# mLSTM attention, router, MoE and MLP in one kernel: the outputs, gates, rows and states of an attention unit taken up one unit later, its turn two units later, and the router's tables built ahead of all units

## The chip, the cores and the metric

The kernel runs on one core of a Trainium2 chip. The metric is the device time of one execution in microseconds (us), as the median of several runs; lower is better. Engines are named as in the profile: PE multiplies matrices (PEld is its weight load, which overlaps), DVE is the vector engine, ACT the scalar engine, POOL the general engine, SP issues most of the loads.

## The reference

Three stages stand one behind the other. The first is a recurrent attention over 4 batches, 8 heads, 768 steps and head size 40, the second a mixture of 8 experts with a capacity, the third a two-layer network.

```python
for t in range(S):                                   # attention
    m_new = np.maximum(f_gate[:, :, t] + m, i_gate[:, :, t])
    f_stab = np.exp(f_gate[:, :, t] + m - m_new); i_stab = np.exp(i_gate[:, :, t] - m_new)
    C = f_stab * C + i_stab * einsum('bhd,bhe->bhde', vt, kt)
    n = f_stab * n + i_stab * kt
    denom = np.maximum(np.abs(einsum('bhd,bhd->bh', n, qt)), 1.0)
    y[:, :, t] = sigmoid(o_gate[:, :, t]) * einsum('bhde,bhe->bhd', C, qt) / denom
logits = x @ w_gate                                  # x: 3072 tokens x 320
# tokens go to experts in the order of falling logits, 384 to an expert
out[mask] = np.maximum(x[mask] @ w1[e], 0.0) @ w2[e]
h = x @ w_in                                         # 320 -> 2048
return np.where(h > 0, h, np.exp(np.minimum(h, 0)) - 1) @ w_out
```

(Broadcast indices are left out.)

## The kernel before

The attention works chunk by chunk: 12 chunks of 64 steps, and for each chunk two pairs of batches, which makes 24 units, `u` = 0 to 23. A unit holds 64 steps of two batches (the two halves of the 128 partitions) and all 8 heads. `Attention.run` (from L455) is one Python loop over the units, and since the schedule is manual each engine executes its instructions in the order in which this loop issues them. That order is the subject of the change.

In one turn of the loop, in order:

- PE: `values(u)` (L368, 32 small matmuls of P and the values into the PSUM tile pO), interleaved with `scores(u+2)` (L283, into pS); then `recall(u)` (L382, the state times the queries, added onto the same pO), interleaved with `state(u)` (L394, new state increments into pC); then `turn(u-1)`: three 128x128 transposes of the output rows x of the unit before into pX (L438), which ACT copies to xT (L440).
- For the next unit: `scan` (DVE, W, L309), `factors` (POOL, vp and qt, L316 and L319), `opens` (ACT, sg is the sigmoid of the output gate, L354), `weigh` (DVE, P is pS times W, L359).
- `gates(u)`: DVE forms 1/max(|n·q|, 1) from the last column of pO (rd, L414, L416, L418), POOL multiplies sg by it (L420). Then `fade(u+1)` on POOL (kt, L328, and the faded state, L330), `decay(u+2)` on PE (pF and pD, L291; ACT copies pD to db, L302).
- `logits(u-1)`: PE multiplies xT by the router's gate weights (L448, six passes), ACT copies 8 columns into L (L449). `add_state(u)`: DVE adds pC to the state C (L405).
- `rows_out(u)`: DVE forms x = pO · sg (L427), ACT pads it (L429) and issues two DMAs of the rows to the DRAM buffer xd (L432, queued on ACT).

Between these stand *fills*: `fl(i)` issues a number of conversion pieces of the later network's weights `w_in` (list FP, from unit 4 on) and of steps of the router's early work (list EP). A piece of `w_in` is loaded by SP into cx; ACT takes an absolute value (cg, L868), DVE does three bit operations on it (cF, L873, L877, L880, the last one with cg as input), then ACT and POOL (L926, L928) or ACT and DVE (wis, L932 to L938) split it into two parts. The router's early work (`Router.early`, DVE, L608 to L628) takes the logits of six units' rows at a time for a first digit of the threshold search; `Router.tables` makes constant tables with iotas on POOL (L517 to L543) and shifts on DVE (from L547).

PSUM holds eight tiles here: pO and pS have two buffers each, pF, pD, pC and pX one each. A matmul that writes a buffer waits until the reader of what stood in it is done.

After the last unit come `turn(23)`, `logits(23)` and the last early work; then the router's search over all 3072 tokens, a chain of DVE and PE steps that needs all of L, and with its first indices the gather of rows from xd. The rest of the span, from about 200 us on, is the experts and the network, ordered by a planner; the change doesn't touch that.

Of the kernel before, what the change touches and what calls it, by code (L numbers as in the profile page):

```python
# [8 lines left out]
F32 = mybir.dt.float32  # L9
# [8 lines left out]
NS, NU = 12, 24  # L18
# [16 lines left out]
class Plan:  # L35
# [3 lines left out]
    def __init__(self):  # L39
        self.n = 0  # L40
        self.todo = []
        self.reset()
# [39 lines left out]
    def next(self):  # L82
        self.due(min(self.todo)[0])
# [30 lines left out]
class Attention:  # L114
# [3 lines left out]

    def __init__(self, nc, tc, consts, qk, vk, ig, fg, wg, xd, L, ident):
        self.nc, self.tc, self.qk, self.vk, self.xd, self.L, self.ident = nc, tc, qk, vk, xd, L, ident  # L120
# [50 lines left out]
        for x in self.CS[0] + self.CS[1]:  # L171
            G.memset(x[:, :, 41:], 0.0)
        self.dp = one.tile([96, S], BF, name="dp")
        self.isT = one.tile([128, NS, 16], F32, name="isT")
# [177 lines left out]
    def opens(self, u):  # L352
        sg = self.st["sg", u] = self.two.tile([128, 8, 40], F32, name="sg")
        self.nc.scalar.activation(sg, self.by_token(u, 2), AF.Sigmoid)  # L354
# [79 lines left out]
    def turn(self, u):  # L434
        x = self.st.pop(("x", u))
        p = self.st["T", u] = self.psum("pX", 1).rearrange("p h t -> p (h t)")
        for k in range(3):
            self.nc.tensor.transpose(p[:, k * 128:k * 128 + 128], x[:, k * 128:k * 128 + 128], self.ident)  # L438
        xT = self.st["xT", u] = self.two.tile([128, 3, 128], F32, name="xT")
        self.nc.scalar.activation(xT.rearrange("p k t -> p (k t)"), p[:, :384], AF.Copy)  # L440

    def logits(self, u):

        l = self.st.pop(("T", u))[:, 384:392]
        x = self.st.pop(("xT", u))
        for k in range(3):
            z = 128 if k < 2 else 64
            self.nc.tensor.matmul(l, x[:z, k], self.wg[:z, k], start=k == 0, stop=k == 2)  # L448
        self.nc.scalar.activation(self.L[:, :, u % 4 * 6 + u // 4], l, AF.Copy)  # L449
# [6 lines left out]
    def run(self, hook, fill):  # L456
        later = self.later()
        for u in range(NU):
            v, w = u + 1, u + 2
            fl = lambda i: ([fill() for _ in range(FP[i])] if u > FU else []) + [self.step() for _ in range(EP[i])]  # L460
            if u % 2 == 0 and u // 2 + 2 < NS:
                self.load_qk(u // 2 + 2)
                self.load_vk(u // 2 + 2)
            self.both(self.values(u), self.scores(w))
            self.both(self.recall(u), self.state(u))
            if u > 0:
                self.turn(u - 1)
            if v < NU:
                self.scan(v)
                self.factors(v)  # L470
                self.opens(v)
                self.weigh(v)
            fl(0)
            if u < 3:
                next(later, None)
            self.gates(u, fl)
            if v < NU:
                self.fade(v)
            fl(2)
            if w < NU:  # L480
                self.decay(w)
            if u > 0:
                self.logits(u - 1)
            self.add_state(u)
            fl(3)
            if u == NU - 1:
                while self.extra:
                    self.step()
            self.rows_out(u)
            fl(4)  # L490
            if u == 0:
                self.turn_gi(2, NS)
                self.keep_gi(2, NS)
            hook(u)
        self.turn(u)
        self.logits(u)
        hook(NU)
        self.es.close()


class Router:
# [9 lines left out]
    def tables(self):  # L511
# [33 lines left out]
        self.thr0 = stage.tile([128, 128], I32, name="thr0", bufs=1)  # L545
        m = stage.tile([128, 128], I32, name="tblt", bufs=1)
        V.tensor_scalar(jt, jt, 25, None, op0=ALU.logical_shift_left)  # L547
        yield
# [854 lines left out]
def kernel(ctx, tc, qk, vk, ig, fg, wg, w1a, w1b, w2a, win, wout, out):  # L1403
# [13 lines left out]
    sp = stage.enter_context(tc.tile_pool(name="cv", bufs=2))  # L1417
    at = Attention(nc, tc, consts, qk, vk, ig, fg, wg, xd, L, ident)

# [5 lines left out]
    def hook(u):  # L1425
        if u == FU:
            fill()
            fill()
        if u == 2:
            rt.__init__(nc, tc, consts, wk, L, sp, plan)  # L1430
            at.extra.append(rt.tables())
            at.step()
        if 4 <= u < 23 and u % 4 == 0:
            at.extra.append(rt.early(u // 4 - 1))
        if u == 22:
            at.extra.append(rt.early(5, 0, 2))
        if u == 23:
            at.extra.append(rt.early(5, 2, 3))
        if u == 24:
            while at.extra:  # L1440
                at.step()
            rt.dg = rt.digits(0)
            for _ in rt.early(5, 3, 4, rt.dg):
                pass
# [18 lines left out]
def _layout(i):  # L1463
# [21 lines left out]
    wg = i["moe_w_gate"][:, ::-1]  # L1485
    d["wg"] = np.concatenate([wg, np.zeros((64, 8), wg.dtype)]).reshape(3, 128, 8).transpose(1, 0, 2)
    d["w1a"] = i["moe_w1"][:, :256].reshape(2048, 1024)
# [22 lines left out]
```

## Time and profile before

| What | Value |
|---|---|
| median of 3 runs | 817.9 us (817.57 to 819.57) |
| the profiled execution's own time | 817.59 us |
| its span, first to last instruction | 815.8 us |
| mean granted TensorE clock | 0.925 of full |
| busy, share of the span: PE, DVE, ACT, POOL | 89%, 72%, 43%, 38% |
| attention's units by the first `values` matmul (L368) | 12.67 us (unit 0) to 157.09 us (unit 23) |

The busy shares are a mean over stages with different limits: PE's 89% comes from the long part behind 200 us. In the 24 units that the change reorders the shares are others and differ among themselves, so the rows further down are taken stage by stage. A stretch named by two units runs from the first `values` matmul of the one to that of the other. Where a row names "issue" as what was waited for, the profile shows nothing else that the engine waited for.

### The profile page before, as it was taken

Reading aid. Unit: us, or ns where it says so; the run is one execution under the profiler, and the core shown is the slowest. Engines: PE = TensorE matmul, PEld = TensorE weight load, DVE = VectorE, ACT = ScalarE, POOL = GpSimd, SP = SyncE. Lnnn points to the kernel's source line nnn. Section 1 sums busy time; section 2 is a strip of 40 time slices with the busy share of each in tenths; the row PEclk is TensorE's granted clock in tenths of the full one; section 3 lists DMA queues with packets and bytes.
Section 4 is the critical chain, followed back from the end, with each engine's and each line's share of the span. In section 5 each row is a group of like instructions: output and inputs, shape, how many; then the busy total and the mean of one; then the engine's idle time right before and its main releaser. Section 6 shows DMA issues by size and latency. Waiting matters only on the chain.

```text
span 815.8 us, 18330 instructions
## 1 busy us (share of the span) xinstructions
PE 729.8 (89%) x7355; PEld 681.9 (84%) x7355; DVE 586.1 (72%) x1616; ACT 348.5 (43%) x743; POOL 309.2 (38%) x358
## 2 busy tenths in 40 slices
PE   7788788836899799799999999999999999999995
PEld 5678678725788789789989988898999999999995
DVE  8697878777979976987897679867733942862542
ACT  5343334324356533543553255325533633742431
POOL 3687887626425631633134125213410601201001
PEclk8678787856999999999999999999999999999998
DMA  8766855135114202112123103200500410100000
GB/s 343 253 216 209 278 186 187 43 107 199 54 30 139 83 27 78 51 44 100 32 65 93 40 0 106 67 27 0 172 12 13 138 35 25 65 1 26 1 1 25
DMA packets 20757, 72.79 MB, mean 89 GB/s; under 512 B 3200, under 2 KB 7296, under 8 KB 19264
## 3 DMA queue, kind: packets, MB, share of 16 engines
q1 hardware_dynamic: 8336, 35.08, 12.6%
q0 software_dynamic: 8448, 31.73, 11.8%
q10 hardware_dynamic: 3888, 4.82, 2.1%
q8 instruction: 58, 0.95, 0.5%
q14 instruction: 27, 0.22, 0.1%
HBM read 62.96 MB, written 8.65 MB: 88 GB/s over the span
## 4 chain that ended last, share of the span: by engine, by line
PE 58%; DVE 21%; issue 8%; ACT 4%; DMA 4%; POOL 2%; ACTq 1%; SPq 0%; POOLq 0%; DVEq 0%
PE ph L1096 24%; PE acc L1234 5%; PE acc L1238 4%; PE acc L1235 4%; PE acc L1203 3%; PE acc L1205 3%; PE acc L1204 3%; DVE e L1149 2%; DMA xd<-x 2%; PE pr L727 2%; DVE ge L713 1%; DVE gl L980 1%; PE acc L1190 1%; PE pX L448 1%; DMA vk<-in_vk_dram 1%
## 5 line engine op out<-in xcount | busy, mean ns | idle before, releaser
L1234 PE MATMUL acc<-woh,gh 128*128 128x320 f32 x384 | 122.7, 320 | 0.0
L1238 PE MATMUL acc<-woh,gl 128*128 128x320 f32 x384 | 119.7, 312 | 0.0
L1235 PE MATMUL acc<-wol,gh 128*128 128x320 f32 x384 | 119.0, 310 | 0.0
L1149 DVE SCALAR_TENSOR_TENSOR e<-e,ph 128x384 f32<-128x384 f32 x128 | 69.9, 549 | 61.8 <-ACT e L1146 61.4
L1145 ACT ACTIVATE e<-ph 128x384 f32<-128x384 f32 x128 | 62.7, 489 | 116.3 <-PE ph L1096 112.0
L980 POOL TENSOR_TENSOR gl<-e,gh 128x384 fp32r<-128x384 f32 x33 | 34.8, 1057 | 164.3 <-DVE gh L974 132.3
L1096 PE MATMUL ph<-yh,wih 128*128 128x384 f32 x256 | 89.7, 351 | 0.4
L1096 PE MATMUL ph<-yh,wil 128*128 128x384 f32 x256 | 86.2, 337 | 0.0
L1113 ACT ACTIVATE gh<-ph 128x384 fp32r<-128x384 f32 x64 | 31.3, 491 | 121.9 <-PE ph L1096 120.7
L1244 POOL DMA_INDIRECT out_dram<-ot,idx x24 | 24.0, 1001 | 141.3 <-ACT ot L972 138.1
L1120 DVE SCALAR_TENSOR_TENSOR gl<-ph,gh 128x384 fp32r<-128x384 f32 x64 | 35.4, 556 | 56.8 <-ACT gh L1113 56.4
L1238 PEld LDWEIGHTS acc<-woh,gl 128*128 128x128 f32 x384 | 72.5, 189 | 0.6
L1234 PEld LDWEIGHTS acc<-woh,gh 128*128 128x128 f32 x384 | 72.8, 190 | 0.2
L1235 PEld LDWEIGHTS acc<-wol,gh 128*128 128x128 f32 x384 | 72.7, 189 | 0.0
L1146 ACT ACTIVATE e<-e 128x384 f32<-128x384 f32 x128 | 67.3, 526 | 4.0
L1096 PE MATMUL ph<-yl,wih 128*128 128x384 f32 x256 | 66.5, 341 | 0.0
L980 DVE TENSOR_TENSOR gl<-e,gh 128x384 fp32r<-128x384 f32 x95 | 57.3, 607 | 1.9
L1096 PEld LDWEIGHTS ph<-yh,wih 128*128 128x128 f32 x256 | 48.4, 189 | 4.5 <-ACT yh L1208 4.4
L1096 PEld LDWEIGHTS ph<-yh,wil 128*128 128x128 f32 x256 | 48.3, 189 | 0.0
L1096 PEld LDWEIGHTS ph<-yl,wih 128*128 128x128 f32 x256 | 46.4, 189 | 0.0
L1096 PE MATMUL ph<-xh,w1h 128*128 128x384 f32 x128 | 45.0, 352 | 0.2
L1203 PE MATMUL acc<-gh,w 128*128 128x384 f32 x128 | 44.6, 349 | 0.0
(269 smaller groups left out, 2023.5 us busy)
## 6 DMA issues: line engine op xcount, KB each, us to landing
vk<-in_vk_dram SPq DMA_DIRECT2D x12, 968.0 KB, 8.7
qk<-in_qk_dram SPq DMA_DIRECT2D x11, 1024.0 KB, 8.0
wx<-in_wout_dram SPq DMA_DIRECT2D x16, 320.0 KB, 2.8
xd<-x ACTq DMA_DIRECT2D x48, 96.0 KB, 3.7
cx<-in_win_dram SPq DMA_DIRECT2D x8, 512.0 KB, 4.4
qk<-in_qk_dram SPq DMA_DIRECT2D x2, 512.0 KB, 5.9
cx<-in_win_dram SPq DMA_DIRECT2D x4, 256.0 KB, 4.2
xg<-xd,idx POOLq DMA_INDIRECT x24, 3.3
```

Source lines behind the costliest of these rows:

```text
L980: (self.nc.vector if e == "d" else self.nc.gpsimd).tensor_tensor(out, x, y, op=ALU.subtract)
L1096: PE.matmul(p, w, x, start=k == 0, stop=k == 7)
L1113: nc.scalar.activation(h, p, AF.Relu)
L1120: nc.vector.scalar_tensor_tensor(l, p, 0.0, h, op0=ALU.max, op1=ALU.subtract)
L1145: nc.scalar.activation(e, p, AF.Relu, scale=-1.0)
L1146: nc.scalar.activation(e, e, AF.Exp, scale=-1.0)
L1149: nc.vector.scalar_tensor_tensor(e, e, -1.0, p, op0=ALU.add, op1=ALU.max)
L1203: PE.matmul(p, w[:, c], h, start=f == 0, stop=False)
L1204: PE.matmul(p, w[:, cl], h, start=False, stop=False)
L1234: PE.matmul(p, h[:, c], self.woh[:, f], start=f == 0, stop=False)
L1235: PE.matmul(p, h[:, c], self.wol[:, f], start=False, stop=False)
L1238: PE.matmul(p, l[:, c], self.woh[:, f], start=False, stop=f == 15)
```

## The change

In the turn of the loop for unit u, `add_state`, `gates` and `rows_out` are now those of unit u-1, `turn` and `logits` those of unit u-2; `add_state(u-1)` is the first thing in the turn. `values`, `recall`, `state`, `scan`, `factors`, `opens`, `weigh`, `fade` and `decay` stay. What is left over follows the loop: gates and rows of unit 23, then turn and logits of 22 and 23, the last one in a buffer of pS. sg gets a third buffer. The third transpose reads columns 192 to 319 of x rather than the padded columns 256 to 383, and the gate weights' rows are laid out to match. The iotas on POOL are issued while the attention is set up, before unit 0, and no longer in unit 2; each part of the router's early work starts one unit later.

```diff
@@ Attention.__init__
+        next(tables)
@@ opens
-        sg = ... self.two.tile([128, 8, 40], F32, name="sg")
+        sg = ... self.two.tile([128, 8, 40], F32, name="sg", bufs=3)
@@ turn
-        p = ... self.psum("pX", 1)
+        p = ... self.psum(*(("pX", 1) if u < NU - 1 else ("pS", 2)))
         for k in range(3):
-            transpose(p[:, k * 128:k * 128 + 128], x[:, k * 128:k * 128 + 128], self.ident)
+            c = min(k * 128, 192)
+            transpose(p[:, k * 128:k * 128 + 128], x[:, c:c + 128], self.ident)
@@ logits
-            z = 128 if k < 2 else 64
-            matmul(l, x[:z, k], self.wg[:z, k], start=k == 0, stop=k == 2)
+            z = 0 if k < 2 else 64
+            matmul(l, x[z:, k], self.wg[z:, k], start=k == 0, stop=k == 2)
@@ run
         for u in range(NU):
+            if u > 0:
+                self.add_state(u - 1)
...
             self.both(self.recall(u), self.state(u))
-            if u > 0:
-                self.turn(u - 1)
+            if u > 1:
+                self.turn(u - 2)
...
-            self.gates(u, fl)
+            if u > 0:
+                self.gates(u - 1, fl)
...
-            if u > 0:
-                self.logits(u - 1)
-            self.add_state(u)
-            fl(3)
-            if u == NU - 1:
-                while self.extra:
-                    self.step()
-            self.rows_out(u)
+            if u > 1:
+                self.logits(u - 2)
+            fl(3)
+            if u > 0:
+                self.rows_out(u - 1)
...
-        self.turn(u)
-        self.logits(u)
-        hook(NU)
+        self.gates(u, lambda i: self.step())
+        while self.extra:
+            self.step()
+        self.rows_out(u)
+        for k in (u - 1, u):
+            self.turn(k)
+            self.logits(k)
+            hook(k + 2)
@@ hook
-        if 4 <= u < 23 and u % 4 == 0:
+        if 5 <= u < 23 and u % 4 == 1:
             at.extra.append(rt.early(u // 4 - 1))
-        if u == 22:
+        if u == 23:
             at.extra.append(rt.early(5, 0, 2))
...
```

The order of the instructions at two places shows what that does. In its rows a tile's name carries a number that tells one buffer's use from the next, and the end names the engines or queues whose semaphores an instruction waits for.

The first place is DVE in unit 7. Before, pO_1163 is the output tile of unit 7 itself and x_1281 its rows:

```order
L309 SCALAR_TENSOR_TENSOR W_1235<-pF_1128,id8_135 128x512 [waits PE_49]
L359 TENSOR_TENSOR P_1242<-pS_1037,W_1235 128x512 [waits DVE_49]
L873 TENSOR_SCALAR cF_982<-cx_980 128x512 [waits DMAHW0_49]
L414 TENSOR_SCALAR rd_1246<-pO_1163 128x8 [waits PE_49]
L877 SCALAR_TENSOR_TENSOR cF_982<-cx_980,cF_982 128x512 [waits DVE_49]
L416 TENSOR_TENSOR rd_1246<-rd_1246,pO_1163 128x8 [waits DVE_49]
L418 RECIPROCAL rd_1246<-rd_1246 128x8 [waits DVE_49]
L405 TENSOR_TENSOR C11_143<-C11_143,pC_153 128x8x41 [waits PE_49,Pool_49]
L880 SCALAR_TENSOR_TENSOR cF_982<-cg_981,cF_982 128x512 [waits Activation_49]
L427 TENSOR_TENSOR x_1281<-pO_1163,sg_1113 128x320 [waits DMAHW3_49,DMAHW1_49,Pool_49]
```

After, pO_1006 is the output tile of unit 6, and x_1260 that unit's rows (its line numbers are 1 higher here, 8 higher in the conversions):

```order
L406 TENSOR_TENSOR C01_140<-C01_140,pC_184 128x8x41 [waits PE_49]
L310 SCALAR_TENSOR_TENSOR W_1214<-pF_1105,id8_135 128x512 [waits PE_49]
L360 TENSOR_TENSOR P_1221<-pS_1007,W_1214 128x512 [waits DVE_49]
L881 TENSOR_SCALAR cF_962<-cx_960 128x512 [waits DMAHW6_49]
L415 TENSOR_SCALAR rd_1225<-pO_1006 128x8
L885 SCALAR_TENSOR_TENSOR cF_962<-cx_960,cF_962 128x512 [waits DVE_49]
L636 TENSOR_TENSOR A_1093<-w8_163,a8_1092 128x32
L417 TENSOR_TENSOR rd_1225<-rd_1225,pO_1006 128x8 [waits DVE_49]
L419 RECIPROCAL rd_1225<-rd_1225 128x8 [waits DVE_49]
L888 SCALAR_TENSOR_TENSOR cF_962<-cg_961,cF_962 128x512 [waits Activation_49]
L428 TENSOR_TENSOR x_1260<-pO_1006,sg_953 128x320 [waits DMAHW7_49,DMAHW1_49,Pool_49]
```

The state's addition moved to the head, and rd no longer waits for PE. The reader that frees unit 6's output tile, x_1260, now stands at the end of unit 7 behind the conversion that waits for ACT; the tile that takes the same buffer is that of unit 8, whose `values` are PE's next instructions.

The second place is ACT at the end of the attention. Before, from the logits copy of unit 21 to that of unit 23:

```order
L449 ACTIVATE L_70<-pX_3101 128x8 [waits PE_49]
L429 ACTIVATE x_3126<-x_3126 128x64 [waits DMAHW7_49,DMAHW6_49,DVE_49]
L432 DMA xd_71<-x_3126 64x384 [waits Activation_49]
L432 DMA xd_71<-x_3126 64x384
L440 ACTIVATE xT_3168<-pX_3164 128x384 [waits PE_49]
L449 ACTIVATE L_70<-pX_3164 128x8 [waits PE_49]
L429 ACTIVATE x_3186<-x_3186 128x64 [waits DMAHW1_49,DMAHW0_49,DVE_49]
L432 DMA xd_71<-x_3186 64x384 [waits Activation_49]
L432 DMA xd_71<-x_3186 64x384
L440 ACTIVATE xT_3195<-pX_3191 128x384 [waits PE_49]
L449 ACTIVATE L_70<-pX_3191 128x8 [waits PE_49]
```

After, from the turned rows of unit 21 to the logits copy of unit 23:

```order
L442 ACTIVATE xT_3147<-pX_3143 128x384 [waits PE_49]
L451 ACTIVATE L_70<-pX_3143 128x8 [waits PE_49]
L430 ACTIVATE x_3159<-x_3159 128x64 [waits DMAHW7_49,DMAHW6_49,DVE_49]
L433 DMA xd_71<-x_3159 64x384 [waits Activation_49]
L433 DMA xd_71<-x_3159 64x384
L430 ACTIVATE x_3176<-x_3176 128x64 [waits DMAHW1_49,DMAHW0_49,DVE_49]
L433 DMA xd_71<-x_3176 64x384 [waits Activation_49]
L433 DMA xd_71<-x_3176 64x384
L442 ACTIVATE xT_3185<-pX_3181 128x384 [waits PE_49]
L451 ACTIVATE L_70<-pX_3181 128x8 [waits PE_49]
L442 ACTIVATE xT_3201<-pS_3197 128x384 [waits PE_49]
L451 ACTIVATE L_70<-pS_3197 128x8 [waits PE_49]
```

Behind PE's last `recall` there were two copies to xT and two to L, those of units 22 and 23; now there are three of each, and the pads and DMAs of units 22 and 23 stand ahead of the last two pairs.

## Rows read from the trace of the kernel before

**Rows 1.** The first line of the page.

```profile
span 815.8 us, 18330 instructions
```

**Rows 2.** Busy time of the engines in five stretches: units 0 to 3 and the first third of the next, then to unit 14, to unit 19, to unit 21, and the end of the attention. Columns: the window's start and end, its length, busy us of PE, PEld, DVE, ACT and POOL (with instructions), PE's granted clock, the DMA engines' share, GB/s.

```profile
12.67:46.67 34.00, 27.25 (x745) 25.50 (x742) 25.14 (x54) 15.33 (x35) 20.34 (x39) 0.72 0.71 255
46.67:117.76 71.09, 58.42 (x1685) 53.96 (x1684) 59.96 (x116) 27.12 (x71) 59.55 (x62) 0.76 0.71 234
117.76:143.46 25.70, 20.84 (x614) 18.99 (x613) 21.52 (x44) 10.82 (x27) 19.39 (x21) 0.80 0.58 198
143.46:157.09 13.63, 11.48 (x381) 10.48 (x380) 12.28 (x29) 5.43 (x16) 11.85 (x14) 1.00 0.20 48
157.09:167.00 9.91, 8.13 (x100) 7.04 (x100) 3.60 (x17) 1.96 (x7) 1.33 (x2) 0.55 0.18 42
```

**Rows 3.** What PE waited for from 42.67 us to 157.09 us (the start of unit 4 to that of unit 23): waiting line, releaser, us in total, times, longest us.

```profile
PE pC L394 <- POOL kt L328: 5.2, 6, 1.7
PE pO L382 <- issue: 4.8, 3, 2.4
PE pX L448 <- ACT xT L440: 2.1, 4, 1.0
PE pC L394 <- issue: 1.8, 2, 1.2
PE pD L291 <- issue: 1.7, 2, 1.0
PE pF L291 <- DVE W L309: 1.0, 2, 0.6
```

**Rows 4.** The same for DVE, in the same stretch.

```profile
DVE rd L414 <- PE pO L382: 6.5, 4, 3.5
DVE x L427 <- POOL sg L420: 3.8, 7, 0.7
...
```

**Rows 5.** The timeline of PE, ACT and DVE at the end of unit 7: start, length, engine, instruction, and in brackets the engine's idle time before it and its releaser.

```profile
65.89 0.55 PE L438 MATMUL pX<-ident,x 128*128 128x128 f32 x3
67.02 0.93 PE L448 MATMUL pX<-wg,xT 128*128 128x8 f32 x6
67.88 0.27 PE L368 MATMUL pO<-vp,P 64*64 64x64 f32 x2
...
66.48 0.49 ACT L440 ACTIVATE xT<-pX 128x384 f32<-128x384 f32 x1 [4.47 <-PE pX L438]
66.86 0.46 ACT L354 ACTIVATE sg<-vk 128x320 f32<-128x320 f32 x1
67.22 0.66 ACT L868 ACTIVATE cg<-cx 128x512 f32<-128x512 f32 x1
...
67.92 1.27 DVE L880 SCALAR_TENSOR_TENSOR cF<-cg,cF 128x512 int32<-128x512 int32 x1 [0.47 <-ACT cg L868]
69.11 0.48 DVE L427 TENSOR_TENSOR x<-pO,sg 128x320 f32<-128x320 f32 x1
```

**Rows 6.** The same at the end of unit 13.

```profile
105.57 0.66 ACT L868 ACTIVATE cg<-cx 128x512 f32<-128x512 f32 x1
...
106.26 1.01 DVE L880 SCALAR_TENSOR_TENSOR cF<-cg,cF 128x512 int32<-128x512 int32 x1 [0.58 <-ACT cg L868]
...
106.91 0.37 PE L368 MATMUL pO<-vp,P 64*64 64x64 f32 x2
```

**Rows 7.** The same at the end of unit 19.

```profile
142.92 0.63 ACT L934 ACTIVATE wis<-cF 64x512 fp32r<-64x512 f32 x1
...
143.96 1.01 DVE L938 TENSOR_TENSOR wis<-cF,wis 64x512 fp32r<-64x512 f32 x1
...
143.46 0.27 PE L368 MATMUL pO<-vp,P 64*64 64x64 f32 x2
```

**Rows 8.** The end of the attention. First five pieces of the chain that ended last, in order of time (start, length, what); then from the timeline, in its form, two instructions of DVE and the two DMAs on ACT's queue.

```profile
160.00 0.84 PE pX L438 x3
160.87 0.50 ACT xT L440
161.41 1.56 PE pX L448 x6
163.08 0.27 ACT x L429
...
166.63 0.20 ACT L L449
...
160.12 0.17 DVE L608 TENSOR_REDUCE b<-L 128x2 f32<-128x16 f32 x1
161.67 0.49 DVE L427 TENSOR_TENSOR x<-pO,sg 128x320 f32<-128x320 f32 x1
163.36 1.10 ACTq L432 DMA_DIRECT2D xd<-x  x2
```

**Rows 9.** What PE waited for from 12 us to 42.67 us, in the form of group 3; one line of it.

```profile
PE pX L438 <- ACT isT L250: 1.7, 1, 1.7
```

**Rows 10.** The timeline of POOL at the start of the attention and of DVE where the router's tables are made.

```profile
11.59 0.74 POOL L316 TENSOR_TENSOR vp<-vk,isT 128x328 f32<-128x328 f32 x1 [7.96 <-DMA vk<-in_vk_dram]
...
37.09 0.26 DVE L547 TENSOR_SCALAR jt<-jt 128x128 int32<-128x128 int32 x1 [3.48 <-POOL jt L534]
```

**Rows 11.** The queue of the page's third part that carries instructions: packets, MB, share of 16 engines.

```profile
q8 instruction: 58, 0.95, 0.5%
```

More of the change, by code (lines that the diff above doesn't have):

```diff
@@ L114, with __init__ @@
 class Attention:
-    def __init__(self, nc, tc, consts, qk, vk, ig, fg, wg, xd, L, ident):
+    def __init__(self, nc, tc, consts, qk, vk, ig, fg, wg, xd, L, ident, tables):
         self.nc, self.tc, self.qk, self.vk, self.xd, self.L, self.ident = nc, tc, qk, vk, xd, L, ident
@@ L352, in opens @@
     def opens(self, u):
-        sg = self.st["sg", u] = self.two.tile([128, 8, 40], F32, name="sg")
+        sg = self.st["sg", u] = self.two.tile([128, 8, 40], F32, name="sg", bufs=3)
         self.nc.scalar.activation(sg, self.by_token(u, 2), AF.Sigmoid)
@@ L435, in turn @@
         x = self.st.pop(("x", u))
-        p = self.st["T", u] = self.psum("pX", 1).rearrange("p h t -> p (h t)")
+        p = self.st["T", u] = self.psum(*(("pX", 1) if u < NU - 1 else ("pS", 2))).rearrange("p h t -> p (h t)")
         for k in range(3):
-            self.nc.tensor.transpose(p[:, k * 128:k * 128 + 128], x[:, k * 128:k * 128 + 128], self.ident)
+            c = min(k * 128, 192)
+            self.nc.tensor.transpose(p[:, k * 128:k * 128 + 128], x[:, c:c + 128], self.ident)
         xT = self.st["xT", u] = self.two.tile([128, 3, 128], F32, name="xT")
@@ L446, in logits @@
         for k in range(3):
-            z = 128 if k < 2 else 64
-            self.nc.tensor.matmul(l, x[:z, k], self.wg[:z, k], start=k == 0, stop=k == 2)
+            z = 0 if k < 2 else 64
+            self.nc.tensor.matmul(l, x[z:, k], self.wg[z:, k], start=k == 0, stop=k == 2)
         self.nc.scalar.activation(self.L[:, :, u % 4 * 6 + u // 4], l, AF.Copy)
@@ L546, in tables @@
         m = stage.tile([128, 128], I32, name="tblt", bufs=1)
+        yield
         V.tensor_scalar(jt, jt, 25, None, op0=ALU.logical_shift_left)
@@ L1417 @@
     sp = stage.enter_context(tc.tile_pool(name="cv", bufs=2))
-    at = Attention(nc, tc, consts, qk, vk, ig, fg, wg, xd, L, ident)
+    rt.__init__(nc, tc, consts, wk, L, sp, plan)
+    tables = rt.tables()
+    at = Attention(nc, tc, consts, qk, vk, ig, fg, wg, xd, L, ident, tables)
     wp = m.win_pieces(sp)
@@ L1429, in hook @@
         if u == 2:
-            rt.__init__(nc, tc, consts, wk, L, sp, plan)
-            at.extra.append(rt.tables())
+            at.extra.append(tables)
             at.step()
-        if 4 <= u < 23 and u % 4 == 0:
+        if 5 <= u < 23 and u % 4 == 1:
             at.extra.append(rt.early(u // 4 - 1))
-        if u == 22:
+        if u == 23:
             at.extra.append(rt.early(5, 0, 2))
-        if u == 23:
-            at.extra.append(rt.early(5, 2, 3))
         if u == 24:
-            while at.extra:
-                at.step()
+            for _ in rt.early(5, 2, 3):
+                pass
+        if u == 25:
             rt.dg = rt.digits(0)
@@ L1485, in _layout @@
     wg = i["moe_w_gate"][:, ::-1]
-    d["wg"] = np.concatenate([wg, np.zeros((64, 8), wg.dtype)]).reshape(3, 128, 8).transpose(1, 0, 2)
+    d["wg"] = np.concatenate([wg[:256], np.zeros((64, 8), wg.dtype), wg[256:]]).reshape(3, 128, 8).transpose(1, 0, 2)
     d["w1a"] = i["moe_w1"][:, :256].reshape(2048, 1024)
```

## The prediction

> **What bounds the kernel now.** First the page's head: the profiled execution took 817.59 us, its span is 815.8 us [rows 1], so 1.8 us lie around the span, and it stands 0.3 us below the median of 817.9. The sum below is made against 817.6. PE's 89% of the span is no use for this change, because most of it comes from the stage behind the attention; so I took the busy time stage by stage [rows 2]. The reader is to see that in none of the attention's stretches an engine is full: from 46.67 to 117.76 us DVE works 59.96, POOL 59.55 and PE 58.42 of 71.09 us; the same holds from 117.76 to 143.46. In such a stretch the time is made by who waits for whom. So the next view was the list of waits. PE waited 5.2 us for kt of POOL, 2.1 for xT of ACT, 1.0 for W of DVE, and 8.3 us (4.8 + 1.8 + 1.7) stand as "issue", for which the profile names nothing in this kernel [rows 3]. DVE waited 6.5 us, its longest wait 3.5, for `recall` of the unit itself before it could make rd [rows 4]. That is a ring: PE's recall, DVE's rd, POOL's sg, POOL's kt behind it, PE's state. The last views are the timelines: two units' ends, with who stands where [rows 5, 6], a third one [rows 7], and the attention's end, where every step is on the path [rows 8].
>
> **The ring, opened.** With gates one unit later rd finds pO ready and DVE's 6.5 us of waiting for PE go. Nothing on PE waited for rd itself; what it gives PE is an earlier sg on POOL and so an earlier kt. I credit all of PE's wait for kt, 5.2 us [rows 3]; the bounds are 0 and 5.2. PE's waits for xT (2.1) and W (1.0) I leave: turn and xT keep their place behind recall in the unit, and W now stands behind one more DVE operation, the state's addition. One more gap, the 1.0 us that is the longest "issue" ahead of pD [rows 3], lies ahead of a place where PE will wait anyway (next part), and I take 1.0 off for it.
>
> **A new wait at each conversion unit.** pO has two buffers. `values(u+1)` overwrites the tile of unit u-1, and its last reader is now x(u-1), which moved to the end of DVE's unit u. Before, that tile had been read a whole unit earlier, so PE never had to wait there. Whether it does now depends on what stands ahead of x. In unit 7 that is the last bit operation of a conversion, which waits for cg of ACT; cg stands behind xT and sg on ACT's queue, and xT waits for PE's turn, which starts only after recall. That part of the chain keeps its place in the change. Its rows [rows 5]: turn 65.89, xT 66.48, sg 66.86, cg 67.22 + 0.66, the conversion 67.92 + 1.27, x 69.11 + 0.48 = 69.59. PE's own work after recall (turn, pF, pD, logits) ends where `values` of unit 8 began, at 67.88. So PE would wait 69.59 − 67.88 = 1.71 us. In unit 13 the conversion ends at 106.26 + 1.01 = 107.27; x would follow it as in unit 7, starting 0.08 before its end, for 0.48, and end at 107.67; `values` began at 106.91 [rows 6], so 0.76. PE's steps are longer there (the first `values` 0.37 against 0.27 in unit 8), DVE's are not. In unit 19 the wait is for the split on ACT: 142.92 + 0.63 = 143.55, then 1.01 and 0.49 less the overlap make about 145.0, against 143.46 [rows 7]: 1.55. The mean is 1.34. The pieces fall so that such an operation stands right ahead of x in eight units (4, 7, 10, 13, 16, 18 with cg, 17 and 19 with the split): 8 × 1.34 = 10.7 us added. Behind the waiting `values` all of PE's queue is held: scores, recall, state, the next turn. The bounds are 8 × 0.76 = 6.1 and 8 × 1.71 = 13.7. In the other units x ends earlier than PE's own work, since nothing ahead of it waits for ACT, and POOL's sg now starts earlier.
>
> A rule speaks against counting only eight. The Trainium skill (Perfetto Trace Analysis, Optimization Strategy) says that one gap that repeats on the engine that should be full can mean too few buffers for the next tile. The trace of before shows no wait of `values`; by that rule each of the units 4 to 22 would have it, which is the fourth rival below.
>
> **The attention's end.** Call the end of the last recall T, 160.00 [rows 8]. Before, from T on: turn 0.84, xT 0.50, logits 1.56 of unit 22, then the same again behind ACT's pad and DMAs, and L of unit 23 done at 166.83 (166.63 + 0.20), T + 6.83. The router needs it, so each added us here counts in full. After, unit 21's turn, xT, logits, L come first: 0.84 + 0.50 + 1.56 and L, with the small gaps between them T + 3.2. On DVE the step that waits for that L (the L608 of before) stands between the parts of rd(23). In before x of unit 23 ended 162.16, 2.04 after that step began at 160.12; so now T + 5.25. ACT then pads it (0.27) and issues two DMAs (1.10): T + 6.7. Only behind them, in ACT's order, comes xT of unit 22 (0.50), though its turn was done before; then logits 1.56, on PE turn of unit 23 (0.84) behind that, xT 0.50, logits 1.56, L 0.20. With the gaps seen in before: T + 12.05. So 12.05 − 6.83 = +5.2 us. The granted clock is 0.55 in this stretch [rows 2]; at the full clock turn and logits take 0.55 and 0.93 [rows 5], and the sum would be about +4.3.
>
> **The start.** The turn in unit 1 goes, and with it its wait of 1.7 us for isT [rows 9]; turn and logits of unit 0 leave unit 1 too (0.55 + 0.93), so at most 3.2. But `values` of unit 2 now needs x of unit 0, which comes late; I take −1.5, near the wait itself; the bounds are 0 and −3.2.
>
> **The tables.** Their iotas cost POOL some 3.5 us, by DVE's wait for them of 3.48 [rows 10]. Before unit 0 POOL sits idle 7.96 us until the values arrive at 11.59 [rows 10], which hides them; and where they stood PE did not stop for POOL. I take 0, bounds +1.2 (if they outlast the idle time) and −1.0. The third sg buffer and the narrower reading of x cost no instruction.
>
> **Sum:** 817.6 − 5.2 − 1.0 + 10.7 + 5.2 − 1.5 = 825.8, so 826 us, slower by 1%.
>
> The Trainium skill (Runtime: NRT & Kernel Launch, Instruction fetch mechanics) says that refilling an engine's instructions block by block is mostly hidden. The trace has 58 such packets, 0.95 MB, which is 16 KB each [rows 11], beside the 8.3 us of "issue" [rows 3], and so rather shows fetches that are not hidden; I leave those gaps. If the rule held, they would be waits of another kind that an order can remove, and 825.8 − 8.3 gives 817.5, in the second rival's range.
>
> **Rivals.** *Second: the new stalls only take the place of other waits.* A PE that stands at `values` gives POOL, ACT and DVE time, so that the waits for kt, xT and W all go (8.3 us), and every other stall falls together with one of them, so that half are left, 5.3: 817.6 − 8.3 + 5.3 + 5.2 − 1.5 − 1.0 = 817.3. For it speaks that the sum of waits on PE is as large as the stalls; against it, that they lie at other places in the unit. Chance 0.17.
>
> *Third: faster.* DVE's waits for PE were the ring, and without it the stretches from 46.67 to 143.46 shrink towards what DVE must do: 59.96 of 71.09 and 21.52 of 25.70 [rows 2], 15.3 us less, of which DVE's waits for sg (3.8) stay: −11.5. With tail and start 817.6 − 11.5 + 5.2 − 1.5 = 809.8. It needs a PE that does its 58.42 us without the waits, at a clock that stands above 0.76 when its gaps close: the granted clock is 1.00 from 143.46 to 157.09 [rows 2], where the loads have ended. Against it: PE's work plus its "issue" gaps alone nearly fill these stretches. Chance 0.22.
>
> *Fourth, part of slower:* every unit from 4 to 22 stalls, 19 × 1.34 = 25.5 in place of 10.7: about 840. It would need x late also where nothing before it waits for ACT, and the trace has none such. Chance 0.05.
>
> **How the numbers follow.** The forecast has a chance of 0.56. Its own range takes the stalls at 0.76 each, the tail at +4.3 and all credits: 817.6 + 6.1 + 4.3 − 7.7 = 820.3; and at the other end the stalls at 1.71, the tail at +5.2 and half the kt credit: 817.6 + 13.7 + 5.2 − 2.6 = 833.9. The rivals below it reach to 809.8. So the range is 810 to 834, which leaves out the fourth rival and the lower half of the third. A measurement of this kernel tells 0.3% (2.45 us) from no change. Slower by more: 0.56 + 0.05 = 0.61; within it: 0.17; faster: 0.22.
>
> **What would show it.** In the profile after: a wait of PE at `values` (L369) for x of DVE, none before, in units 8, 14 and 20, of 0.8 to 1.7 us, and about 11 us in all; PE's wait for kt gone; DVE's wait of rd for recall gone up to unit 22; L of unit 23 done 12 us after the last recall, with xT of unit 22 started behind four DMA issues; POOL's iotas before 11.59. Were the wait at `values` absent, the time would be 815 and the forecast wrong in its main term; were it there at every unit, wrong the other way; were the tail's rise under 2 us, the order on ACT was not what decides there.

## The result and the profile after

The changed kernel took 830.38 us in the median of four runs (825.82 to 831.38), the kernel before 818.74 us beside it: a ratio of 1.0139, 95% interval 1.009 to 1.0188. Run once more on another chip it gave 1.0117 (1.008 to 1.0155). The forecast, 825.8 of 817.6, is 1.010. So the change makes the kernel slower, by a little more than was forecast and inside the range.

The profiled execution of the changed kernel is at the upper end of its runs (831.29 us, span 829.5), 13.7 us above that of before. Its windows answer to [rows 2]; the columns are the same. They begin where units 0, 5, 16, 20 and 23 begin, and so do those of [rows 2], whose heading names the units wrongly.

```profile
span 829.5 us, 18239 instructions
```

```profile
12.74:46.41 33.67, 27.34 (x731) 25.57 (x728) 26.09 (x52) 15.10 (x35) 19.59 (x24) 0.70 0.66 250
46.41:120.24 73.83, 60.52 (x1683) 56.97 (x1684) 57.21 (x118) 26.63 (x69) 57.56 (x61) 0.70 0.66 226
120.24:151.09 30.85, 21.80 (x613) 20.48 (x612) 21.70 (x44) 11.17 (x29) 20.74 (x24) 0.72 0.44 163
151.09:164.41 13.32, 12.71 (x379) 11.83 (x380) 10.75 (x30) 4.46 (x13) 8.54 (x10) 0.87 0.20 48
164.41:177.60 13.19, 8.44 (x105) 7.13 (x105) 3.75 (x18) 2.80 (x10) 1.59 (x2) 0.67 0.20 47
```

The first stretch is 0.3 us shorter than before, the second 2.7 us longer, the third 5.1 us longer, the fourth 0.3 us shorter, and the last, from unit 23 to just behind its logits, 3.3 us longer. What PE waited for in units 4 to 22 answers to [rows 3]:

```profile
PE pO L369 <- DVE x L428: 11.9, 8, 3.5
PE pO L383 <- issue: 3.6, 3, 1.4
PE pD L292 <- issue: 3.2, 1, 3.2
PE pF L292 <- issue: 2.0, 1, 2.0
PE pO L369 <- issue: 1.2, 1, 1.2
...
PE pX L450 <- ACT xT L442: 0.6, 1, 0.6
```

The waits for kt (5.2) and W (1.0) are gone, and that for xT fell from 2.1 to 0.6. In their place PE stands 11.9 us at `values` for x of DVE, where it never stood before; one more stop, at unit 2, makes it 12.4 in nine stops. The second change is on DVE: it no longer waits for `recall`, as in [rows 4], but runs ahead and waits for ACT. These are its waits from 12 to 170 us:

```profile
DVE cF L888 <- ACT cg L876: 12.8, 4, 5.5
DVE x L428 <- POOL sg L421: 10.7, 14, 1.2
...
DVE wis L946 <- ACT wis L942: 5.8, 2, 3.3
```

The longest stop of PE, 3.45 us ahead of unit 11, shows what holds it. The timeline of unit 10, PE first, then ACT, DVE and POOL:

```profile
83.57 0.93 PE L450 MATMUL pX<-wg,xT 128*128 128x8 f32 x6
87.94 0.37 PE L369 MATMUL pO<-vp,P 64*64 64x64 f32 x2 [3.45 <-DVE x L428]
...
83.77 0.67 ACT L876 ACTIVATE cg<-cx 128x512 f32<-128x512 f32 x1
...
83.50 1.65 DVE L885 SCALAR_TENSOR_TENSOR cF<-cx,cF 128x512 int32<-128x512 int32 x1
...
85.68 0.68 DVE L888 SCALAR_TENSOR_TENSOR cF<-cg,cF 128x512 int32<-128x512 int32 x1
86.28 1.21 DVE L628 TENSOR_TENSOR g<-b,thr 128x512 bf16<-128x512 f32 x1
87.41 0.48 DVE L428 TENSOR_TENSOR x<-pO,sg 128x320 f32<-128x320 f32 x1
...
85.72 1.22 POOL L421 TENSOR_TENSOR sg<-sg,rd 128x320 f32<-128x320 f32 x1 [1.12 <-DVE rd L419]
```

PE's own work ends at 84.50. x, the last reader of the buffer that `values` wants, starts at 87.41 behind a whole conversion and, what the prediction had not seen, four steps of the router's early work, one of 1.21 us. POOL's sg, which x needs too, ends at 86.94, since rd stands behind the same conversion. Here cg is not what is late (it was done at 84.44), DVE is: a conversion step took 1.65 us.

The attention's end, on ACT, answers to [rows 8]; recall of unit 23 ended at 166.49.

```profile
167.01 0.49 ACT L442 ACTIVATE xT<-pX 128x384 f32<-128x384 f32 x1 [2.14 <-PE pX L440]
168.51 0.19 ACT L451 ACTIVATE L<-pX 128x8 f32<-128x8 f32 x1 [1.02 <-PE pX L450]
...
171.11 1.10 ACTq L433 DMA_DIRECT2D xd<-x  x2
172.25 0.49 ACT L442 ACTIVATE xT<-pX 128x384 f32<-128x384 f32 x1 [1.18 <-issue]
...
177.34 0.19 ACT L451 ACTIVATE L<-pS 128x8 f32<-128x8 f32 x1 [1.63 <-PE pS L450]
```

L of unit 23 is done at 177.53, T + 11.04, against T + 6.83 before: +4.2 us. What this is measured against moves with the granted clock: the end in its old order took 6.83 us here at a clock of 0.50, but 5.95 at 0.85 (run 8) and 5.33 at 1.00 (the tables alone, run 3), while the new end took 11.0 in six profiles, at 0.61 to 0.74. So the end costs 4.2 to 5.7 us.

**Where the 13.7 us are.** Units 0 to 22 take 151.67 us instead of 144.42: +7.25, of which +2.9 is PE's idle time and +4.4 PE's busy time at a lower granted clock (0.72 against 0.78). Unit 23 up to the end of recall takes 2.08 instead of 2.91, and the end +4.2. That is 10.7 at L of unit 23. These are figures of single executions: in two more profiles with the same lags (runs 3 and 4) units 0 to 22 take 147.66 and 149.49 us, of which PE is busy 116.86 and 117.90, no more than the 118.00 of before. The other 3.0 us come after it, in three jumps of about 0.9 us, near 196, 280 and 347 us of before; they are taken up below.

### The profile page after: what moved, and what is told of

It is laid out like the page before. It is cut to its first block, busy times and chain, and to the rows that moved or that the text cites. A ratio compares the mean times of both kernels' runs of the same rounds, so it can differ in the third digit from the quotient of the medians.

```text
span 829.5 us, 18239 instructions
## 1 busy us (share of the span) xinstructions
PE 737.1 (89%) x7355; PEld 690.7 (83%) x7355; DVE 583.9 (70%) x1616; ACT 348.1 (42%) x743; POOL 309.8 (37%) x358
## 3 DMA queue, kind: packets, MB, share of 16 engines
q1 hardware_dynamic: 8336, 35.08, 11.9%
## 4 chain that ended last, share of the span: by engine, by line
PE 53%; DVE 16%; issue 6%; ACT 3%; DMA 1%; POOL 0%; POOLq 0%; ACTq 0%; DVEq 0%
PE ph L1104 24%; PE acc L1242 5%; PE acc L1246 4%; PE acc L1243 4%; PE acc L1211 3%; PE acc L1213 3%; PE acc L1212 3%; DVE e L1157 2%; PE pr L735 2%; DVE gl L988 1%; PE acc L1198 1%; DVE ge L721 1%; PE acc L1200 1%; PE ph L1057 1%; ACT e L1153 1%
## 5 line engine op out<-in xcount | busy, mean ns | idle before, releaser
L369 PE MATMUL pO<-vp,P 64*64 64x64 f32 x768 | 39.8, 278 | 13.6 <-DVE x L428 12.4
L369 PEld LDWEIGHTS pO<-vp,P 64*64 64x64 f32 x768 | 35.6, 185 | 14.9 <-DVE x L428 13.2
```

What stands on the lines that cost most here:

```text
L369: self.nc.tensor.matmul(o[64 - r:128 - r, h], P[r:r + 64, h], self.VP[u % 2][r:r + 64, h], start=h == 0, stop=n == 0 and h == 7)
```

## The experiments

The runs came in groups, each group on a chip of its own with the kernel before beside it; its median was 818.14, 822.94, 820.91 and 819.46 us there. So ratios are compared, not times; a ratio is the recorded one with its 95% interval, and it differs from the quotient of the two medians by up to 0.3%.

**1. x ahead of the last conversion piece.** After, with:

```diff
-            fl(3)
             if u > 0:
                 self.rows_out(u - 1)
+            fl(3)
             fl(4)
```

> The changed kernel with one thing moved: the rows x of unit u-1 (with their pad and DMAs) are issued ahead of the last conversion piece and router step of the unit, not behind them. Theory A (PE's wait at values is made by the conversion and the router's step that stand ahead of x on DVE, and the lower granted clock of units 0 to 22, 0.72 against 0.78, comes from these stops): PE's wait at values for x falls from 12.4 us to under 4, the clock in units 0 to 22 goes back to 0.76 or more, and the time is 815 to 821 us. Rival B (something must wait there anyway; with the conversion now ahead of the state's addition, W and P the wait only moves to P): PE waits at values for P or at state for C, 8 us or more, and the time stays at 826 or more.

Measured: 823.22 us (819.82 to 828.45), ratio 1.0079 (1.0049 to 1.0109). Its waits of PE:

```profile
PE pO L369 <- DVE x L428: 6.5, 7, 1.4
...
PE pC L395 <- DVE C L406: 2.9, 4, 1.5
```

Half of each theory: about half of the wait at `values` goes, and part of it comes back at `state`, which waits for the state's addition. That addition opens DVE's next unit, behind the conversion piece that now follows x. On the same chip the lags without this move gave 1.0142 (run 3). The clock of units 0 to 22 is 0.75, which the changed kernel has too in its second profile (run 4), so this rise cannot be put down to the move.

**2. The lag given up at the end.** After, with the end as before and unit 22 catching up:

```diff
...
+            if u == NU - 2:
+                self.turn(u - 1)
+                self.gates(u, lambda i: None)
+                self.logits(u - 1)
+            if u >= NU - 2:
+                self.rows_out(u)
...
```

> The changed kernel with the lag given up at the end: unit 22 also takes up its own gates and rows and the turn and logits of unit 21, unit 23 its own gates and rows and the turn of 22, as in the kernel before. Theory A (the third turn, copy and logits behind the last recall cost 4 us in full): L of unit 23 is done 6.8 us after the last recall instead of 11.0, some 1 us comes back as extra work in unit 22, and the time is 826 to 828 us. Rival B (the router's search or the loads behind it set the end anyway): L is done earlier but the time stays at 829 to 831 us.

Measured: 828.04 us (825.43 to 831.73), ratio 1.0145 (1.0115 to 1.0175): no gain that can be measured. L of unit 23 is done 6.07 us after the last recall, as hoped; but PE's timeline shows what unit 22 pays ahead of `values` of unit 23:

```profile
158.70 0.55 PE L440 MATMUL pX<-ident,x 128*128 128x128 f32 x3 [0.28 <-ACT L L451]
160.52 1.55 PE L450 MATMUL pX<-wg,xT 128*128 128x8 f32 x6 [1.27 <-ACT xT L442]
162.00 0.37 PE L369 MATMUL pO<-vp,P 64*64 64x64 f32 x2
```

The second turn, the wait for its copy and the second logits stand in line for 3.3 us, and unit 22 takes 7.65 us instead of 4.00. More is paid in unit 23 up to the end of recall, here and then in the changed kernel (columns as in [rows 2]):

```profile
162.00:165.68 3.68, 3.68 (x66) 3.56 (x66) 0.00 (x0) 0.35 (x2) 0.00 (x0) 0.50 0.24 58
164.41:166.49 2.08, 2.08 (x66) 2.01 (x66) 0.65 (x2) 0.34 (x2) 0.72 (x1) 1.00 0.24 55
```

The same `values` and `recall` take 1.6 us longer, at a granted clock of 0.50 in place of 1.00. So the 5.0 us saved at the end are paid in full ahead of it; the 1 us of extra work in Theory A was too little.

**3. The tables alone, and the lag alone.** The first is before with `next(tables)` ahead of unit 0, the second after without it.

> The kernel before with the router's iotas issued ahead of unit 0 and nothing else changed. Theory A (POOL stands idle 8 us there, and PE does not wait for POOL where the iotas stood): 817 to 820 us, no difference that can be measured. Rival B (the iotas in unit 2 hold up POOL's vp, kt and C of the next units): faster by 2 us or more, 816.5 us or less.

Measured: 817.46 us (815.38 to 821.91), ratio 1.0008 (0.9985 to 1.003).

> The changed kernel with the router's iotas issued in unit 2 as before. Theory A (the lag alone makes the loss): 829 to 832 us, as the changed kernel. Rival B (the early tables carry part of the loss or of a gain at the start): 827 us or less, or 833 us or more.

Measured: 827.48 us (826.69 to 829.88), ratio 1.0142 (1.0114 to 1.017); the time lies between the two theories' limits, the ratio is that of the changed kernel. The tables carry none of the loss that these intervals can show.

**4. The changed kernel again, and a copy that frees the buffer.**

> The changed kernel itself once more, as the base for the other runs of this group on the same chip. Expected 826 to 832 us, a ratio of about 1.014, with 11 to 14 us of PE's wait at values for x; the parts of the spread that come from the granted clock show in the clock of units 0 to 22 (0.72 in the first profile).

Measured: 833.03 us (831.86 to 834.89), ratio 1.0117. PE waits 13.5 us for x, in ten stops. PE's busy time in units 0 to 22 is 117.90 us here, as in the kernel before (118.00), not 122.36: the lower clock of the first profile is not a fixed price of the change.

```diff
+    def copy_out(self, u):
+        o = self.two.tile([128, 8, 41], F32, name="oc")
+        self.nc.scalar.activation(o, self.st["O", u][:, :, :41], AF.Copy)
+        self.st["O", u] = o
```

> The changed kernel with one addition: behind the turn ACT copies the output tile pO (328 columns) to a tile of its own in the other memory, from which rd and x read, so that pO is free soon after recall, whatever stands ahead of x on DVE. It adds 24 ACT copies of about 0.5 us. Theory A (the loss is pO's two buffers held by a late x): PE's wait at values for DVE's x is gone and no other takes its place, the time is 816 to 821 us. Rival B (DVE or ACT as such cannot keep up with a unit, so PE must wait once per unit wherever the buffer is freed): 6 us or more of PE waits for DVE or ACT appear at values, state or pF, and the time stays at 825 or more.

Measured: 834.49 us (833.0 to 836.68), ratio 1.013 (1.0093 to 1.0168): nothing gained. The wait for x is gone; these are PE's wait that took its place, and, from the view of one line, the durations of x (least, median, most, in ns):

```profile
PE pC L395 <- DVE C L406: 6.5, 5, 2.8
```

```profile
L433 DVE TENSOR_TENSOR x<-oc,sg x24: 491/1009/1595, 24.1 to 172.4; 128x320 f32<-128x320 f32 x24
```

A free output buffer does not help, since pC, the tile of the state's increments, has one buffer, and its reader is late for the same reason: all that DVE issues in a unit must be done before the next one's first instruction. That wait is about half of the one that went; PE is also busy 127.57 us in units 0 to 22, at a clock of 0.70, and why was not tried. And x itself, 477 to 493 ns in the changed kernel, takes 1009 ns in the median once both its inputs come from SBUF instead of one from PSUM. The trace tells when: the 21 that ran beside an instruction of POOL took 916 to 1595 ns, and the last three, with POOL idle, 491 to 493; in the changed kernel x takes its 0.49 us beside POOL's kt as well. The Trainium skill (SBUF — State Buffer, SBUF: two separate sides) says that DVE and POOL share a pair of ports there, which a DVE operation with two SBUF inputs can lose to POOL for a whole instruction. The trace agrees. The prediction quotes the rule of the Trainium skill (Perfetto Trace Analysis, Optimization Strategy) that repeated gaps can mean too few buffers. It is met here only in part: one more buffer moves the gap to the next single one.

**5. The gates first, then also the state's addition in its old place.** Gates of u-1 go to the head of unit u, x right behind P; in the second kernel the addition returns to its unit:

```diff
             if u > 0:
                 self.add_state(u - 1)
+                self.gates(u - 1, lambda i: None)
...
+            if u > 0:
+                self.x_out(u - 1)
             fl(0)
...
```

```diff
-                self.add_state(u - 1)
...
                 self.logits(u - 2)
+            self.add_state(u)
             fl(3)
```

> The changed kernel with gates of u-1 taken up at the head of unit u, with the state's addition, and the product x right behind P of unit u+1, ahead of all conversion pieces and router steps; its pad and DMAs stay where they were. Theory A (what stands between the head of the unit and x makes the wait): PE's wait at values for x is under 1.5 us in all, the time 815 to 820 us, and better than with x moved alone (823.2), where rd and sg still stood behind two conversion steps. Rival B (DVE's work per unit is what PE waits for): waits for P or C appear instead, 5 us or more, and the time is 822 us or more.

Measured: 827.55 us (824.89 to 836.47), ratio 1.0067 (1.0035 to 1.0099). The wait for x is gone; at `state` stands the rival's, 7.3 us in five stops. The time is above Theory A's, and the ratio cannot be told from that of run 1. PE, then DVE:

```profile
91.34 0.33 PE L395 MATMUL pC<-vp,kt 64*40 64x64 f32 x2 [2.04 <-DVE rd L415]
...
88.12 1.53 DVE L888 TENSOR_SCALAR cF<-cx 128x512 int32<-128x512 int32 x1
89.68 1.11 DVE L892 SCALAR_TENSOR_TENSOR cF<-cx,cF 128x512 int32<-128x512 int32 x1
90.71 0.48 DVE L406 TENSOR_TENSOR C<-C,pC 128x328 f32<-128x328 f32 x1
```

The view names rd, which ends 0.1 us behind C; that C's place decides is shown by the next kernel, where rd stays.

> The kernel with the gates first (behind it: x ahead of all conversions), and the state's addition of unit u put back to its place of before, in unit u behind the logits. Theory A (with x out of the way the state's addition at the head of DVE's next unit, behind a conversion that waits for ACT, is what state on PE then waits for): PE's wait at state for DVE, 7.3 us with the gates first, is under 1.5 us, and the ratio to the kernel before falls from 1.007 to 1.000 or below (4 us or more less). Rival B (the instruction gaps, which rose from 12.6 to 17.6 us as other waits went, take its place): the waits at state go, 'issue' rises to 20 us or more, and the ratio stays at 1.005 or more.

Measured: 825.04 us (818.48 to 828.9), ratio 1.0035 (1.0004 to 1.0067). PE's waits:

```profile
PE pF L292 <- issue: 7.5, 4, 3.8
PE pO L369 <- issue: 6.5, 2, 3.6
...
PE pO L383 <- issue: 3.3, 3, 1.6
PE pF L292 <- DVE W L310: 3.0, 5, 1.2
```

The wait at `state` falls from 7.3 to 0.9 us. The ratio lies between the two theories' limits, and its interval overlaps that of the gates first alone. Units 4 to 22, where the stops were, tell more than the time. This is that stretch in the kernel before, in the changed one, in this one, and in that of run 6, which has the same order up to unit 23 (columns as in [rows 2]):

```profile
42.67:157.09 114.42, 94.63 (x2829) 87.07 (x2828) 97.68 (x195) 45.10 (x116) 93.39 (x100) 0.81 0.60 198
40.07:164.41 124.34, 100.14 (x2828) 94.08 (x2828) 92.87 (x198) 44.56 (x116) 91.04 (x98) 0.73 0.53 182
38.26:154.08 115.82, 94.09 (x2828) 87.03 (x2828) 101.62 (x195) 43.93 (x116) 92.93 (x100) 0.81 0.58 195
41.59:158.83 117.24, 96.85 (x2828) 90.20 (x2827) 101.84 (x195) 44.10 (x116) 92.26 (x99) 0.75 0.57 193
```

It takes 121.50 and 120.85 us in the two other profiles with the lags alone (runs 4 and 3), 119.39 with the gates first, and 116.72 with the tables alone. So with both releases moved the units take as long as without the lags, as far as this spread of about 2 us lets one see: the loss within them was the place of DVE's two releases. That this order is faster there than the kernel before is not shown: units 0 to 22 take 141.01 us in this profile, at a clock of 0.81, but 145.80 in that of run 6, at 0.73, against 144.42. Rival B is there too: "issue" adds up to 20.3 us in units 0 to 22. What is left of the loss is the end, 11.0 us after the last recall.

> The kernel of the run before, with the lag given up in units 22 and 23. Theory A (both losses are separate and add): 4 us less than with the gates first alone, L of unit 23 done 7 us after the last recall, 811 to 816 us, which would beat the kernel before. Rival B (the catching up in unit 22 costs PE what the end saves, as the first try of the tail suggests): within 1.5 us of the gates first alone.

Measured: 828.80 us (826.2 to 832.27), ratio 1.0072 (1.0043 to 1.0101): Rival B, as in the first try of the tail.

**6. The end, by ACT's order.** The kernel with gates first and the addition put back, and turn and logits of unit 22 ahead of the rows of unit 23:

```diff
+        self.turn(u - 1)
         self.gates(u, lambda i: self.step())
...
+        self.logits(u - 1)
+        hook(u + 1)
         self.rows_out(u)
-        for k in (u - 1, u):
-            self.turn(k)
-            self.logits(k)
-            hook(k + 2)
+        self.turn(u)
+        self.logits(u)
+        hook(u + 2)
```

> The same with one thing more at the end: turn, xT and logits of unit 22 ahead of the pad and DMAs of unit 23's rows on ACT. Theory A (the place of xT of unit 22 behind two pads and four DMA issues costs its wait of 2.7 us): L of unit 23 is done 8.0 to 9.0 us after the last recall, not 11.0, and the time is 2 to 3 us lower than with the gates and the addition alone. Rival B (the conversion of unit 22's logits then holds up rows or steps that the end also needs): 10.5 us or more after the last recall.

Measured: 824.65 us (820.72 to 828.63), ratio 1.0028 (1.0003 to 1.0054). ACT after the last recall, which ended at 160.91:

```profile
164.46 0.49 ACT L445 ACTIVATE xT<-pX 128x384 f32<-128x384 f32 x1 [1.18 <-PE pX L443]
...
166.97 1.10 ACTq L436 DMA_DIRECT2D xd<-x  x2
168.12 0.49 ACT L445 ACTIVATE xT<-pS 128x384 f32<-128x384 f32 x1 [1.18 <-PE pS L443]
170.24 0.19 ACT L454 ACTIVATE L<-pS 128x8 f32<-128x8 f32 x1 [1.64 <-PE pS L453]
```

L is done at T + 9.52, between the two theories: xT of unit 22 no longer stands behind unit 23's DMAs, but xT of unit 23 now does. The order on ACT costs 1.5 us, not 2 to 3; in the time that cannot be told from nothing.

**7. The turn's lag alone.** Before, with only turn and logits two units later, and the router's steps as these need them:

> The kernel before with turn and logits two units later and the third turn at the end, and nothing else of the change but the router's early steps, which then must start one unit later: gates, states and rows stay in their own unit. Theory A (the turn's lag costs only at the end; the rest of the loss is the lag of rows and states): PE has no wait at values for x, the wait for kt stays at 4 to 6 us, L of unit 23 is done 9.5 to 11 us after the last recall, and the ratio is 1.003 to 1.006. Rival B (the turn's lag alone makes the whole loss, by the router's steps in other units): 1.010 or more.

Measured: 823.07 us (821.12 to 829.13), ratio 1.0034 (1.0006 to 1.0063). PE's wait for kt is 5.9 us, there is none at `values` for x, and L of unit 23 is done at T + 8.8, earlier than the 9.5 to 11 expected. So the lag of the turn costs the end and, as far as this interval tells, no more, and the lag of rows and states costs the rest: 1.0139 or 1.0117 for both.

**8. The ring opened without a lag.** Before, with two lines swapped:

```diff
-            self.gates(u, fl)
             if v < NU:
                 self.fade(v)
+            self.gates(u, fl)
```

> The kernel before with one pair swapped on POOL: kt and the faded state of unit u+1 (fade) ahead of the product of sg with rd of unit u. This opens the ring recall, rd, sg, kt, state without any lag, so the end stays as before. Theory A (the waits for kt are all that the lag had to give, and each us of them is worth a us): PE's wait for kt, 5.2 us before, is under 1 us, L of unit 23 is done 6.8 us after the last recall, and the ratio to the kernel before is 0.992 to 0.997. Rival B (instruction gaps, which rose from 12.6 to 20 us when the waits of PE went in other kernels, take the place): the wait for kt goes, 'issue' rises by 4 us or more, and the ratio is 0.998 to 1.002.

Measured: 815.94 us (814.14 to 820.65), ratio 0.9967 (0.9942 to 0.9992), faster than both kernels. PE's waits in units 4 to 22:

```profile
PE pC L394 <- issue: 5.4, 3, 3.5
PE pX L448 <- ACT xT L440: 4.0, 7, 0.7
PE pO L382 <- issue: 3.8, 3, 2.9
PE pF L291 <- DVE W L309: 3.8, 7, 0.6
PE pX L438 <- DVE a L625: 2.1, 3, 1.5
...
```

The wait for kt is gone from the list, and "issue" did not rise (11.1 us in units 0 to 22, 12.6 before). But other waits took its place: those for xT and W make 7.8 us instead of 3.1, and the turn waits 2.1 for DVE (the view names a router's step that stands right behind x). sg now stands behind kt and the faded state on POOL, and DVE's x waits 9.9 us for it, 3.8 before. So PE's idle time in units 4 to 22 did not fall, 21.7 us against 19.8, and these units take 115.7 us, not less than the 114.4 of before. What this profile gains lies elsewhere: 2.7 us in units 0 to 3, where an instruction gap of 2.4 is gone, and 1.7 from unit 23 on, at a higher clock (1.00 and 0.85, for 0.67 and 0.50). The time is that of Theory A, but its reason, that each us of the wait for kt is worth a us, is not shown; the cause of the gain stays open.

## Why the prediction was right, and where its sizes were not

- **The new wait at `values`** was the main term, 10.7 us in eight units. Seven of the eight stops are there, ahead of units 5, 8, 11, 14, 18, 19 and 20, with 11.1 us; the eighth, ahead of unit 17, is covered by an instruction gap of 3.24 us inside unit 16; units 2 and 10 have short ones of 0.4 and 0.9, where x waited 0.8 for POOL's sg. The sum was right with the single sizes off, which is luck in part: 0.42 for the 1.71 ahead of unit 8, where PE, at a clock of 0.50, was late itself; 1.12 for 0.76 ahead of unit 14; 1.63 for 1.55 ahead of unit 20; and 3.45 ahead of unit 11. The prediction told the wait as ACT's cg or split: ahead of six of the seven stops DVE did stand idle for these, 1.5 to 5.5 us. In unit 10 it was the length of DVE's own queue; there, and in unit 18, router steps that the change had shifted one unit on stood ahead of x.
- **What it left out:** the state's addition. It moved to the head of a unit, behind everything of the unit before on DVE, and pC has one buffer. As long as PE stops at `values` this is hidden; runs 1, 4 and 5 uncovered it, 2.9, 6.5 and 7.3 us.
- **The kt credit**, 5.2, was right in full as a wait that goes; that each us of it is a us of time was not shown by run 8. The xT and W credit was put at 0 and came to 2.5. The gap of 1.0 that was to be absorbed was not: "issue" is 12.6 us in units 0 to 22 before and after. (In units 4 to 22 of before it is 10.2 and not the prediction's 8.3; [rows 3] shows neither 1.3 at the logits nor 0.6 at the scores.)
- **The end**, +5.2 us: measured +4.2 in this pair of profiles, 4.2 to 5.7 over all. The step mis-sized is the clock: turn and logits of unit 21 ran at the full one (0.55 and 0.93), which is the +4.3 that the prediction gave for it. xT of unit 22 stood behind the DMAs, as said, and x of unit 23 ended at T + 4.3, not T + 5.25.
- **The start**, −1.5: at unit 4 the kernel is 2.6 us ahead, though PE stopped 0.4 for x of unit 0: the wait for isT went, and instruction gaps moved. Mis-sized by about a microsecond. Unit 4 gives most of it back (6.34 us for 4.00, at a clock of 0.77 for 1.00), 1.1 of it by its stop for x.
- **The tables**, 0: right (run 3); POOL still stands idle 2.5 us ahead of its first vp.
- **Without a term in the sum:** PE's busy time in units 0 to 22, +4.4 us in this profile and none in the next, and the 3.0 behind the attention.
- **The rivals.** The second (stalls only replace waits) is refuted by the interval, and the fourth (every unit) by the nine stops. The third (faster by a higher clock without the ring) did not come true even with the releases in the right place: units 0 to 22 took 141.0 us at a clock of 0.81 in one profile of that order and 145.8 at 0.73 in the other, and both kernels were slower than the one before (1.0035 and 1.0028).
- **Not settled:** 3.0 us of the profiled difference come behind the attention, where the code is the same. From L of unit 23 to the last instruction it takes 649.0 us in the kernel before and 652.0 in the changed one, but 649.5 with x ahead, 650.7 with the tables alone and 655.5 in the changed kernel's second profile. The last was on another chip, on which the kernel before is some 4 us slower as well; on the chip of runs 1 to 3 the stretch took 649.5 to 652.0 with the lags and 650.7 without. The first jump is the gathered tokens (xg), for which PE's load waited 3.4 us and not 2.5. Whether the changed kernel's share is more than chance was not tried.

## What to carry to other kernels

A lag removes a wait for the producer and gives the buffer's release a later place: count for every lagged reader which instructions now stand ahead of it in its engine's queue, and whether the next writer of its buffer comes sooner than these are done. Put the releases first and the work that nobody waits for last. Where a ring runs through one engine's queue, try first to swap two instructions there (a gain of 0.3% here, its cause open, with no price at the loop's end), since each unit of lag is paid once more after the last unit.

## What was not expected of the hardware

PE's "issue" gaps follow one pattern: in the kernel before, the changed one and all of the experiments the gaps above 0.4 us ended 1.2 to 1.7 us after a packet of the instruction queue ([rows 11]) had landed, with one exception at 1.0. Their sum in units 0 to 22 goes with the order: 12.6 us before, 14.9 with the tables alone, 11.1 with kt first, 12.3 to 13.6 in the changed kernel and in runs 1 to 4 with its lags, 17.6 and 18.1 with the gates first, 20.3 and 19.8 with the addition put back too, and 19.7 with the turn's lag alone, though the number of PE's matmuls is the same, 7355. So a part of what an edit takes out of PE's waits can come back as these gaps; that the fetch causes them was not tested by a run that changes it.
